# Weights ahead of values, and two hidden-layer steps ahead of the value products, at the start of a fused attention and ELU kernel

## Chip, cores, metric

One core of one Trainium2 chip. The metric is the device time of one execution in microseconds, median of several; all runs quoted here were fast, at a granted TensorE clock of 0.99 to 1.00 over the span.

## The reference

Sliding-window attention (8 batches, 8 heads, 576 positions, head size 64, window 32 to each side), its output laid out as 4608 tokens of 512, then a two-layer network with ELU:

```python
scores = q @ k.T / sqrt(64); keep |i - j| <= 32; attn = softmax(scores)
x = (attn @ v) as [4608, 512]
h = x @ w_in                       # [4608, 2048]
g = where(h > 0, h, exp(min(h, 0)) - 1)
out = g @ w_out                    # [4608, 512]
```

## The kernel before

A hand-scheduled program. Attention works on "pairs" of query blocks (128 tokens each); a tile of the network is 256 tokens, so two pairs. A **step** (kk) is 256 columns of the hidden layer for one tile: eight matmuls into a PSUM tile (h0 or h1 in turn), exponential on ACT, subtraction of 1, and the ELU on DVE, which reads the PSUM tile a last time. The hidden columns of steps 0 and 1 come from the first quarter of w_in, those of steps 2 and 3 from the second. Steps 0 to 3 work on tile 0 (pairs 0 and 1), steps 4 to 7 on tile 1 (pairs 2 and 3). The parts that the change touches:

```python
    # GpSimd's load queue
    load_w_in(0)
    ...                                   # masks
    for m in (3, 4):
        load_v(0, m)
    load_w_in(1)
    load_w_out(0)
    load_w_out(1)
    ...
    # pairs 2 and 3, hung onto the steps ("mid": behind the step's matmuls, "dve": ahead of them)
    at(0, "mid", scores, 2, "s")
    at(0, "mid", scores, 3, "u")
    for i in (2, 3):
        at(0, "mid", exponential, i)                              # ACT
    for i in (2, 3):
        at(0, "mid", rotate_v, 0, 2, VS - 1, (i - 2,))            # DVE copy of values, 64 partitions over
        at(0, "mid", mask, i)                                     # DVE
        at(1, "mid", idle, (4, 2)[i - 2], "y1")                   # dummy matmuls on a tile of zeros
        at(1, "mid", pv, i)                                       # PE: probabilities x values
        at(2, "dve", normalize, i)                                # DVE
        at(3, "mid", x_transpose, i)                              # PE
        at(3, "mid", x_evac, i, nc.scalar)                        # ACT, PSUM -> xT
    at(1, "end", idle, 1, "y1")
    ...
    def mm1(kk):
        ...                                                       # 8 matmuls
            nc.scalar.activation(e_sb, ps, AX.Exp)
            if kk == 1:
                nc.scalar.activation(m_sb, e_sb, AX.Copy, bias=-1.0)
            else:
                nc.vector.tensor_scalar(m_sb, e_sb, -1.0, None, ALU.add)
    ...
    for kk in range(NSTEP + LAG):
        run(kk, "first")
        if 1 <= kk < NSTEP:
            elu(kk - 1)
        run(kk, "dve")
        if kk < NSTEP:
            mm1(kk)
        run(kk, "mid")
        for n in {2: (), 3: (0, 1), 4: (), 5: (2, 3)}.get(
                kk, (kk - LAG,) if kk >= LAG else ()):
            mm2(n)                                                # output products of step n
        run(kk, "end")
```

The softmax here doesn't subtract the row's maximum and nothing guards it: scores larger than these inputs give would overflow.

Of the kernel before, what the change touches and what calls it, by code (L numbers as in the profile page):

```python
# [21 lines left out]
def kernel(  # L22
# [24 lines left out]
    VS = 5  # L47
# [9 lines left out]
    NSTEP = NT * STEPS  # L57
# [36 lines left out]
    def ps_tile(shape, dt, tag, name):  # L94
        return pools[tag].tile(shape, dt, tag=tag, name=name)
# [42 lines left out]
    def load_v(b, m):  # L138
        lo = 128 * m - WIN
        p0 = max(0, -lo)  # L140
        p1 = min(128, S - lo)
        nc.gpsimd.dma_start(  # L142
            out=V_e[b % 3][p0:p1, m, :, 0:D],
            in_=v[b, :, lo + p0:lo + p1, :].rearrange("h p d -> p h d"))
# [28 lines left out]
    def load_w_in(c):  # L173
        w = D_FF // 4
        nc.gpsimd.dma_start(
            out=w_in_sb[:, :, c * w:(c + 1) * w],
            in_=moe_w_in[:, c * w:(c + 1) * w].rearrange(
                "(o p) f -> p o f", p=128))

    def load_w_out(c):  # L180
        n = NFO // 4
        nc.gpsimd.dma_start(
            out=w_out_sb[:, c * n:(c + 1) * n, :],
            in_=moe_w_out[c * n * 128:(c + 1) * n * 128, :].rearrange(
                "(o p) f -> p o f", p=128))
# [46 lines left out]
    def copy_on(eng, d_, s_):  # L232
        if eng is nc.scalar:
            nc.scalar.copy(d_, s_)  # L234
        else:
            eng.tensor_copy(d_, s_)  # L236
# [169 lines left out]
    for mi in (0, 4):  # L406
# [4 lines left out]
        out=masks[:, 3, :], in_=masks[:, 3, :], compare_op=ALU.is_ge,  # L411
        fill=0.0, base=128 - WIN - 1, pattern=[[0, QB]],
        channel_multiplier=-1)
    for m in (3, 4):
        load_v(0, m)
    load_w_in(1)
    load_w_out(0)
    load_w_out(1)

# [49 lines left out]
    def at(kk, slot, fn, *args):  # L469
        tasks.setdefault((kk, slot), []).append((fn, args))  # L470

    def run(kk, slot):
        for fn, args in tasks.get((kk, slot), ()):
            fn(*args)
# [11 lines left out]
    at(0, "mid", scores, 3, "u")  # L486
    for i in (2, 3):
        at(0, "mid", exponential, i)
    for i in (2, 3):
        at(0, "mid", rotate_v, 0, 2, VS - 1, (i - 2,))  # L490
        at(0, "mid", mask, i)

        at(1, "mid", idle, (4, 2)[i - 2], "y1")
        at(1, "mid", pv, i)
        at(2, "dve", normalize, i)
        at(3, "mid", x_transpose, i)
        at(3, "mid", x_evac, i, nc.scalar)
    at(1, "end", idle, 1, "y1")
    at(4, "dve", swap_pools)

    for part, kq in ((HALF_A, 7), (HALF_B, 15)):
# [20 lines left out]
    for i in range(4, NPAIR):  # L522
        two = i >= FIRST_TWO
        kk, z = begin[i], i % 2 if two else 0
# [5 lines left out]
        n = kk + (3 + z if two else 2)  # L530
# [57 lines left out]
    def mm1(kk):  # L588
        t, s = order[kk]
        h = kk % 2  # L590


        tags = (f"h{h}", "s") if kk == NSTEP - 1 else (f"h{h}",)
        w = FG // len(tags)
        psH[kk], m_t[kk] = [], []
        for z, tag in enumerate(tags):
            ps = ps_tile([128, w, TT], FP32, tag, "ps")
            psH[kk].append(ps)
            for j in range(w):
                fo = s * FG + z * w + j  # L600
                for do in range(NDO):
                    nc.tensor.matmul(  # L602
                        ps[:, j, :],
                        lhsT=w_in_sb[:, do, fo * 128:(fo + 1) * 128],
                        rhs=xT[t][:, :, do, :],
                        start=(do == 0), stop=(do == NDO - 1))
        for z, ps in enumerate(psH[kk]):
            e_sb = mpool.tile([128, w, TT], FP32, tag="e_sb", name="e_sb")
            nc.scalar.activation(e_sb, ps, AX.Exp)  # L609
            m_sb = mpool.tile([128, w, TT], BF16, tag="m_sb", name="m_sb")  # L610
            if kk == 1:

                nc.scalar.activation(m_sb, e_sb, AX.Copy, bias=-1.0)
            else:
                nc.vector.tensor_scalar(m_sb, e_sb, -1.0, None, ALU.add)  # L615
            m_t[kk].append(m_sb)
            if kk == NSTEP - 1:
                elu(kk, z)

    def elu(kk, z=0):  # L620
        if z == 0:
            g_t[kk] = mpool.tile([128, FG, TT], BF16, tag="g_sb", name="g_sb",
                                   bufs=5)
        ps = psH[kk][z]
        w = ps.shape[1]
        nc.vector.scalar_tensor_tensor(  # L626
            g_t[kk][:, z * w:(z + 1) * w, :], ps, 0.0, m_t[kk][z],
            ALU.max, ALU.min)
# [3 lines left out]
    def mm2(kk):  # L632
        t, s = order[kk]
        if s == 0:
            psY[t] = [ps_tile([128, D_MODEL], FP32, g, "psY")
                      for g in (("h2", "t0") if t == 1 else ("y0", "y1"))]
        g_sb = g_t.pop(kk)
        last = t == NT - 1 and s == STEPS - 1
        for ts in range(2):
            for j in range(FG):  # L640
                nc.tensor.matmul(  # L641
                    psY[t][ts],
                    lhsT=g_sb[:, j, ts * 128:(ts + 1) * 128],
                    rhs=w_out_sb[:, s * FG + j, :],
                    start=(s == 0 and j == 0),
                    stop=(s == STEPS - 1 and j == FG - 1))
        if s == STEPS - 1:
            for ts in range(2):
                z = 1 - ts if last else ts
                eng = (nc.scalar, nc.vector)[z]  # L650
                y_sb = opool.tile([128, D_MODEL], FP32, tag=f"y_sb{z}",
                                  name="y_sb")
                copy_on(eng, y_sb, psY[t][ts])
                (nc.scalar if last and ts else nc.sync).dma_start(
                    out_t[t, :, ts, :], y_sb)

    LAG = 2
    for kk in range(NSTEP + LAG):
        run(kk, "first")
        if 1 <= kk < NSTEP:  # L660
            elu(kk - 1)
        run(kk, "dve")
        if kk < NSTEP:
            mm1(kk)
        run(kk, "mid")

        for n in {2: (), 3: (0, 1), 4: (), 5: (2, 3)}.get(
                kk, (kk - LAG,) if kk >= LAG else ()):
            mm2(n)
        run(kk, "end")  # L670
# [30 lines left out]
```

## Time and profile before

| | before |
|---|---|
| time, median of the first 3 runs | 305.85 us (305.50 to 306.12) |
| span of the profiled run | 304.2 us |
| step 0 starts on PE | 15.62 us |
| step 4 starts on PE | 25.05 us |
| **front**: step 4's start minus step 0's | **9.43 us** |
| **tail**: from step 4's start to the end of the span | **279.15 us** |

The prediction below shows the lines of the profile that carry these. Two more, from the timeline of PE in the kernel before (start, length, engine, line, operation, output from inputs, shapes, count; in brackets the idle time before and what ended it), give both ends of the front:

```profile
15.62 1.05 PE L602 MATMUL ps<-xT,w_in_sb 128*128 128x256 bf16 x8 [0.80 <-DMA w_in_sb<-in_moe_w_in_dram]
...
25.05 1.91 PE L602 MATMUL ps<-xT,w_in_sb 128*128 128x256 bf16 x16
```

The single instructions that the prediction counts with took, in the kernel before: eight matmuls of 256 columns 0.87 us (L602, 0.109 each), four of 512 columns 0.86 us (L641, 0.215 each; the dummies have this shape and are counted at 0.216), a subtraction on DVE 433 ns (L615, the mean) and on ACT 0.63 us (L613), an ELU on DVE 686 ns (L626, the mean).

### The profile page before, as it was taken

Reading aid. Unit: us, or ns where it says so; the run is one execution under the profiler, and the core shown is the slowest. Engines: PE = TensorE matmul, PEld = TensorE weight load, DVE = VectorE, ACT = ScalarE, POOL = GpSimd, SP = SyncE. Lnnn points to the kernel's source line nnn. Section 1 sums busy time; section 2 is a strip of 40 time slices with the busy share of each in tenths; the row PEclk is TensorE's granted clock in tenths of the full one; section 3 lists DMA queues with packets and bytes.
Section 4 is the critical chain, followed back from the end, with each engine's and each line's share of the span. In section 5 each row is a group of like instructions: output and inputs, shape, how many; then the busy total and the mean of one; then the engine's idle time right before and its main releaser. Section 6 shows DMA issues by size and latency. Waiting matters only on the chain.

```text
span 304.2 us, 7587 instructions
## 1 busy us (share of the span) xinstructions
PE 291.5 (96%) x3038; PEld 197.2 (65%) x3091; DVE 242.1 (80%) x472; ACT 169.0 (56%) x254; POOL 48.7 (16%) x68
## 2 busy tenths in 40 slices
PE   7799999999999999999999999999999999999994
PEld 2466666677666666666666666666666666666662
DVE  6866687978788887988798879887988787877663
ACT  3654656778664566546754675467545454533431
POOL 8836101820004100230023002300000000000000
PEclk9999999999999999999999999999999999999999
DMA  9999999999765987999799969996921111111011
GB/s 191 180 204 205 187 279 401 305 146 213 157 197 145 296 120 217 229 319 147 168 259 316 169 166 260 326 159 125 272 56 71 35 71 35 72 37 69 4 67 70
DMA packets 91973, 52.81 MB, mean 174 GB/s; under 512 B 76578, under 2 KB 81698, under 8 KB 91938
## 3 DMA queue, kind: packets, MB, share of 16 engines
q1 hardware_dynamic: 47186, 35.48, 43.4%
q0 software_dynamic: 42880, 10.10, 42.8%
q10 hardware_dynamic: 1872, 6.75, 6.0%
q8 instruction: 24, 0.39, 0.6%
q14 instruction: 11, 0.09, 0.1%
HBM read 36.70 MB, written 15.34 MB: 171 GB/s over the span
## 4 chain that ended last, share of the span: by engine, by line
PE 89%; DMA 3%; POOL 2%; DVE 2%; issue 2%; ACT 1%; POOLq 0%; DVEq 0%
PE ps L602 41%; PE psY L641 39%; PE psS L336 4%; PE psS L304 3%; DMA w_in_sb<-in_moe_w_in_dram 3%; PE ptx L279 1%; POOL Ve L142 1%; POOL c L136 1%; PE psXT L357 1%; DVE pm L324 0%; DVE g_sb L626 0%; DVE Vo L153 0%; PE ptx L274 0%; ACT e_sb L609 0%; ACT pu L315 0%
## 5 line engine op out<-in xcount | busy, mean ns | idle before, releaser
L609 ACT ACTIVATE e_sb<-ps 128x512 f32<-128x512 f32 (+1 forms) x145 | 86.3, 595 | 120.0 <-PE ps L602 110.4
L602 PE MATMUL ps<-xT,w_in_sb 128*128 128x256 bf16 x1152 | 149.2, 273 | 0.9 <-DMA w_in_sb<-in_moe_w_in_dram 0.8
L641 PE MATMUL psY<-w_out_sb,g_sb 128*128 128x512 bf16 x526 | 139.1, 379 | 3.1 <-issue 0.8
L602 PEld LDWEIGHTS <-w_in_sb 128*128 128x128 bf16 x1152 | 110.8, 98 | 39.0 <-DMA w_in_sb<-in_moe_w_in_dram 1.3
L626 DVE SCALAR_TENSOR_TENSOR g_sb<-ps,m_sb 128x512 bf16<-128x512 f32 (+1 forms) x145 | 99.4, 686 | 12.6
L615 DVE TENSOR_SCALAR m_sb<-e_sb 128x512 bf16<-128x512 f32 x144 | 62.4, 433 | 38.0 <-ACT e_sb L609 36.2
L641 PEld LDWEIGHTS <-g_sb 128*128 128x128 bf16 x576 | 54.6, 98 | 38.6 <-DVE g_sb L626 0.2
L142 POOL DMA_DIRECT2D Ve<-in_v_dram x40 | 35.3, 892 | 139.5 <-PE psS L336 81.4
L315 ACT ACTIVATE pu<-psS 128x1024 bf16<-128x1024 f32 x36 | 36.5, 1020 | 1.5 <-PE psS L304 1.5
L348 DVE TENSOR_TENSOR x_st<-psS,rc 128x512 bf16<-128x512 f32 x36 | 24.9, 692 | 1.2
L324 DVE TENSOR_TENSOR pm<-pu,masks 128x1024 bf16<-128x1024 bf16 x36 | 24.6, 683 | 0.6 <-ACT pu L315 0.5
L234 ACT CAST qkb<-f 128x768 bf16<-128x768 f32 (+1 forms) x29 | 24.9, 860 | 0.0
L336 PEld LDWEIGHTS <-pm 128*64 128x64 bf16 x576 | 11.1, 110 | 9.9 <-DVE pm L324 8.7
L336 PE MATMUL psS<-Ve,pm 128*64 128x65 bf16 x320 | 13.6, 196 | 0.9 <-ACT pu L315 0.8
L236 DVE COPY y_sb<-psY 128x512 f32<-128x512 f32 x18 | 12.3, 685 | 0.9 <-PE psY L641 0.9
L304 PEld LDWEIGHTS <-kT 64*128 64x128 bf16 x576 | 9.6, 95 | 4.9 <-issue 4.0
L336 PE MATMUL psS<-Vo,pm 128*64 128x65 bf16 x256 | 12.0, 196 | 0.2 <-DVE Vo L153 0.2
L304 PE MATMUL psS<-qT,kT 64*128 64x64 bf16 x576 | 11.8, 191 | 0.5 <-DVE kT L236 0.5
L234 ACT COPY y_sb<-psY 128x512 f32<-128x512 f32 x18 | 10.5, 582 | 2.2 <-PE psY L641 2.2
L153 DVE COPY Vo<-Ve 64x1040 bf16<-64x1040 bf16 x24 | 10.7, 447 | 1.1 <-DMA Ve<-in_v_dram 0.4
L395 PE MATMUL ps_idle<-zeros 128*128 128x512 bf16 x24 | 8.3, 455 | 1.4 <-DVE zeros L194 1.3
L234 ACT COPY qT<-ptx 128x1152 bf16<-128x1152 bf16 (+2 forms) x8 | 7.6, 974 | 3.6 <-PE ptx L279 2.8
(36 smaller groups left out, 71.8 us busy)
## 6 DMA issues: line engine op xcount, KB each, us to landing
out_dram<-y_sb SPq DMA_DIRECT2D x35, 256.0 KB, 3.4
f<-in_q_dram SPq DMA_DIRECT2D x12, 576.0 KB, 6.1
f<-in_k_dram SPq DMA_DIRECT2D x12, 576.0 KB, 8.3
in_dram<-qkb ACTq DMA_DIRECT2D x10, 576.0 KB, 4.3
Ve<-in_v_dram POOLq DMA_DIRECT2D x24, 128.0 KB, 11.6
w_in_sb<-in_moe_w_in_dram POOLq DMA_DIRECT2D x4, 512.0 KB, 9.8
w_out_sb<-in_moe_w_out_dram POOLq DMA_DIRECT2D x4, 512.0 KB, 12.7
Ve<-in_v_dram POOLq DMA_DIRECT2D x16, 96.0 KB, 10.1
```

The costliest lines, as they stand in the source:

```text
L142: nc.gpsimd.dma_start(out=V_e[b % 3][p0:p1, m, :, 0:D], in_=v[b, :, lo + p0:lo + p1, :].rearrange("h p d -> p h d"))
L234: nc.scalar.copy(d_, s_)
L304: nc.tensor.matmul(psS[:, h % 2, hp * 128 + z * QB:hp * 128 + (z + 1) * QB], lhsT=kT[b % 2][base:base + 64, KPAD + hp * S + QB * qb - WIN: ...
L315: nc.scalar.activation(pu, _bap(psS, [psS.ap[0], [1, 1024]]), AX.Exp, scale=SCALE)
L324: nc.vector.tensor_mul(pm, pu, _bap(mm, [mm.ap[0], [0, H], [1, 2 * QB]]))
L336: nc.tensor.matmul(psS[QB * z:QB * (z + 1), par, hp * VD:(hp + 1) * VD], lhsT=pm[:, par * HP + hp, z * QB:(z + 1) * QB], rhs=vv[:, qb // 2 ...
L348: nc.vector.tensor_mul(x_st, _bap(psS, [psS.ap[0], [VD, HP], [512, 2], [1, D]]), _bap(rc, [rc.ap[0], [2, HP], [1, 2], [0, D]]))
L602: nc.tensor.matmul(ps[:, j, :], lhsT=w_in_sb[:, do, fo * 128:(fo + 1) * 128], rhs=xT[t][:, :, do, :], start=(do == 0), stop=(do == NDO - 1))
L609: nc.scalar.activation(e_sb, ps, AX.Exp)
L615: nc.vector.tensor_scalar(m_sb, e_sb, -1.0, None, ALU.add)
L626: nc.vector.scalar_tensor_tensor(g_t[kk][:, z * w:(z + 1) * w, :], ps, 0.0, m_t[kk][z], ALU.max, ALU.min)
L641: nc.tensor.matmul(psY[t][ts], lhsT=g_sb[:, j, ts * 128:(ts + 1) * 128], rhs=w_out_sb[:, s * FG + j, :], start=(s == 0 and j == 0), stop=( ...
```

## The change

Its intent: fill PE's wait for values 3 and 4 with steps 2 and 3, which need no values. For that the second quarter of w_in is loaded ahead of these values, the products of pairs 2 and 3 go behind step 3, and the subtractions of steps 2 and 3 join step 1's on ACT, so that DVE has less to do.

```diff
--- before.py
+++ after.py
@@ -411,9 +411,9 @@
         out=masks[:, 3, :], in_=masks[:, 3, :], compare_op=ALU.is_ge,
         fill=0.0, base=128 - WIN - 1, pattern=[[0, QB]],
         channel_multiplier=-1)
+    load_w_in(1)
     for m in (3, 4):
         load_v(0, m)
-    load_w_in(1)
     load_w_out(0)
     load_w_out(1)

@@ -486,16 +486,19 @@
     at(0, "mid", scores, 3, "u")
     for i in (2, 3):
         at(0, "mid", exponential, i)
+        at(1, "dve" if i == 2 else "mid", mask, i)
+        at(3, "dve", rotate_v, 0, 2, VS - 1, (i - 2,))
+        at(3, "mid", pv, i)
+
+    at(1, "mid", idle, 3, "y1")
+    at(3, "dve", idle, 3, "y1")
     for i in (2, 3):
-        at(0, "mid", rotate_v, 0, 2, VS - 1, (i - 2,))
-        at(0, "mid", mask, i)
-
-        at(1, "mid", idle, (4, 2)[i - 2], "y1")
-        at(1, "mid", pv, i)
-        at(2, "dve", normalize, i)
+        at(3, "mid", normalize, i)
+    at(3, "mid", lambda: elu(2))
+    for i in (2, 3):
+        at(3, "mid", lambda n: mm2(n), i - 2)
         at(3, "mid", x_transpose, i)
         at(3, "mid", x_evac, i, nc.scalar)
-    at(1, "end", idle, 1, "y1")
     at(4, "dve", swap_pools)

     for part, kq in ((HALF_A, 7), (HALF_B, 15)):
@@ -608,7 +611,7 @@
             e_sb = mpool.tile([128, w, TT], FP32, tag="e_sb", name="e_sb")
             nc.scalar.activation(e_sb, ps, AX.Exp)
             m_sb = mpool.tile([128, w, TT], BF16, tag="m_sb", name="m_sb")
-            if kk == 1:
+            if 1 <= kk <= 3:

                 nc.scalar.activation(m_sb, e_sb, AX.Copy, bias=-1.0)
             else:
@@ -657,14 +660,14 @@
     LAG = 2
     for kk in range(NSTEP + LAG):
         run(kk, "first")
-        if 1 <= kk < NSTEP:
+        if 1 <= kk < NSTEP and kk != 3:
             elu(kk - 1)
         run(kk, "dve")
         if kk < NSTEP:
             mm1(kk)
         run(kk, "mid")

-        for n in {2: (), 3: (0, 1), 4: (), 5: (2, 3)}.get(
+        for n in {2: (), 3: (), 4: (), 5: (2, 3)}.get(
                 kk, (kk - LAG,) if kk >= LAG else ()):
             mm2(n)
         run(kk, "end")
```

## The prediction

> **What bounds the kernel now.** I read first the page's totals, then the windows view by stages, then the chain of waits and the timeline between 15 and 26 us, where every instruction that the change moves stands.
>
> ```profile
> PE 291.5 (96%) x3038; PEld 197.2 (65%) x3091; DVE 242.1 (80%) x472; ACT 169.0 (56%) x254; POOL 48.7 (16%) x68
> ```
>
> TensorE (PE) is busy for 96% of the span, so only its holes, and work on it that nobody needs, can be won. The windows view says where the holes are:
>
> ```profile
> core 0: us, PE busy (x) PEld busy (x) DVE busy (x) ACT busy (x) POOL busy (x), PEclk, DMA share, GB/s
> 15.62:25.05 9.43, 9.09 (x117) 6.08 (x120) 7.32 (x15) 5.71 (x9) 3.35 (x5) 1.00 1.24 204
> 25.05:45.00 19.95, 19.50 (x204) 13.25 (x206) 14.17 (x28) 10.14 (x15) 5.10 (x6) 1.00 1.46 222
> 45.00:304.20 259.20, 252.12 (x2576) 172.31 (x2620) 209.07 (x405) 145.15 (x220) 26.72 (x30) 1.00 0.86 168
> ```
>
> From 25.05 us on PE is 97 to 98% busy, and the waits view for PE after 25 us names nothing but 0.8 us of "issue" and 0.2 us for one x_st; the other gaps stand where a matmul record is missing. So the instant at which step 4 (the first step of the second token tile) starts on PE, 25.05 us, sets the end: a shift of that start should reach the end one to one. Before it, the chain is this:
>
> ```profile
> 16.70 0.61 ACT e_sb L609
> ...
> 17.33 0.46 DVE m_sb L615
> ...
> 17.83 0.43 DVE Vo L153
> ...
> 18.29 0.69 DVE pm L324
> ...
> 19.01 0.43 DVE Vo L153
> ...
> 19.48 0.42 PE psS L336 x15
> ...
> 21.14 1.75 PE ps L602 x16
> 22.89 0.59 PE psXT L357 x8
> ...
> 25.21 1.75 PE ps L602 x16
> ```
>
> The values' products (L336) wait for VectorE (DVE), which does one rotation (L153) and one mask (L324) at a time; steps 2 and 3 (L602 x16) come after them, at 20.98 in the timeline, 21.14 as the chain counts. Between the last matmul of step 1 (started at 17.17, eight at 0.109 us, so PE is free at 18.05) and step 4 at 25.05 lie 7.00 us. The work in it that is needed: steps 2 and 3, 1.75; 32 value products, about 0.76; 8 x transposes, 0.44; 8 output products, 1.72; sum 4.67. So 2.33 us are dummies (seven at 0.216, 1.51 us) and holes. **2.33 us is all that the change can win, 0.8% of the time.**
>
> The timeline has the three things that decide, and the DMA view the landing of the weights:
>
> ```profile
> 17.20 1.93 ACT L315 ACTIVATE pu<-psS 128x1024 bf16<-128x1024 f32 x2
> 19.00 0.62 ACT L609 ACTIVATE e_sb<-ps 128x512 f32<-128x512 f32 x1
> 19.65 0.63 ACT L613 ACTIVATE m_sb<-e_sb 128x512 bf16<-128x512 f32 x1
> 20.07 1.28 DVE L626 SCALAR_TENSOR_TENSOR g_sb<-ps,m_sb 128x512 bf16<-128x512 f32 x2
> 23.42 1.07 ACT L234 COPY xT<-psXT 128x512 bf16<-128x512 bf16 x2
> ```
>
> ```profile
> w_in_sb<-in_moe_w_in_dram POOLq DMA_DIRECT2D x1, 512.0 KB, 8.9
> Ve<-in_v_dram POOLq DMA_DIRECT2D x1, 96.0 KB, 7.6
> ```
>
> First: step 1's exponential on ScalarE (ACT) stands behind the two score exponentials, its subtraction ends at 20.28, and only then can the ELU of step 1 run. Second: both transposed x tiles are out of PSUM at 24.49, half a microsecond before step 4 asks for them. Third: w_in's second quarter, issued at 10.99, lands at 19.9 us.
>
> [...]eight of L602 take 0.87 us, four of L641 0.86. [...]the first ELU waits behind two masks until 20.07 though its subtraction was done at 17.79. [...]433 ns for L615 against 686 for L626[...] the subtraction is the cheaper half to give away, and ACT pays more for it (0.63). [...]here the first w_in quarter, v3, v4, second w_in quarter landed in the order of issue, at 15.57, 16.7, 17.8 and 19.9.
>
> **The change, part by part.** The instruction order on each engine, which the built kernel shows, is: PE step 1, 3 dummies, step 2, 3 dummies, step 3, 32 value products, output products of step 0, transposes of pair 2, output products of step 1, transposes of pair 3, step 4. DVE: subtraction 0, ELU 0, both masks, ELU 1, both rotations, normalize 2 and 3, ELU 2 and 3. ACT: exponential and subtraction of steps 1, 2, 3 in turn, then both x evictions.
>
> (a) *The load order.* Removed from ahead of the second quarter are v3 and v4, which took 17.8 - 15.57 = 2.2 us of the queue. It then lands near 19.9 - 2.2 = 17.7, v4 near 19.9. Step 2 may start once ELU 0 has freed its PSUM: DVE runs it at 17.85 instead of behind the masks, so by 18.54. Neither holds it: step 2 starts behind the dummies, 18.05 + 3 x 0.216 = 18.70, against 20.98 now, and ends 19.57.
>
> (b) *Step 3* needs the PSUM of step 1, so ELU 1 must be over. Nothing in the change moves ACT's two score exponentials or the exponential and subtraction behind them: 20.28. ELU 1 then runs 20.32 to 21.01 and step 3 starts at 21.05, though the second dummies end at 20.22. A hole of 0.83 us. Step 3 ends 21.05 + 0.87 = 21.92.
>
> (c) *Value products.* The rotations stand behind ELU 1: 20.95 and 21.4, over at 21.85. So the products run 21.93 to 22.7, without a wait. Before, the second set was over at about 20.65.
>
> (d) *Normalizing and transposing.* Now they hide behind steps 2 and 3. After the change only the output products lie beside them: reciprocal and product of pair 2 at 22.6 to 23.6, of pair 3 to 24.4. PE: output products 0 to 23.57, transposes of pair 2 to 23.85, output products 1 to 24.71, transposes of pair 3 start there. In the timeline an eviction starts 0.42 to 0.44 us after the start of such transposes (41.48 and 41.90; 12.82 and 13.26) and takes 0.59, and 0.05 for the hand-over: step 4 starts at 24.72 + 0.43 + 0.59 + 0.05 = **25.79**. A second hole, of about 0.85 us, which the kernel before doesn't have.
>
> (e) *Three subtractions on ACT* (step 1's was there already, so two are new): two times 0.52 us off DVE, two times 0.65 onto ACT, where they lie at about 20.3 and 22.7, ahead of the evictions at 24.2 and 25.15. Off the path on both engines; without them ELU 2 and 3 would end 1 us later, near 26.6, which would touch step 5 only.
>
> Sum: 25.79 - 25.05 = +0.74 us. Crosscheck by contents: 4.67 needed, 6 x 0.216 = 1.30 of dummies, holes of 0.83 and 0.85, together 7.65 from 18.05, which is 25.70. So one dummy (0.22) and a hole of 0.6 are given up for two holes of 1.7. 305.85 + 0.7 is about 306.5.
>
> **The rivals.** *The fill works.* If the x evictions or ELU 1 come sooner than I reckon, the two holes close: 18.05 + 1.30 + 4.67 = 24.02, one microsecond earlier, 304.8. For it speaks that steps 2 and 3 plainly have nothing to do with the values, and that the old chain runs through v3 and v4. Against it speaks that ELU 1 and the third-pair eviction are waits in the built order, each behind a measured serial run on ACT or DVE. Closing just one gives about 305.7.
>
> *The weights stay late.* If the second quarter gains less than the 2.2 us, or the bigger transfer that now follows the first quarter slows its tail, step 2 waits: landing at 19.9 puts step 2 at 19.95, the dummies to 21.47 and step 3 to 21.5, another 0.4 us: 306.9. A first quarter late by 0.2 moves everything by 0.2. Against it: the landings follow the order of issue here, and step 2 has 1.0 us in hand.
>
> *Later loads.* Reused load semaphores make the third w_in quarter wait for v3 instead of v4, and so issue perhaps 1 us later. The queue is then still full with what was issued before it (that quarter took 12.2 us from issue to landing), and it landed at 30.3 against step 8 at 32.73. Hidden: 0.
>
> **Range and chances.** The centre is my sum, 306.5. The low end, 305.7, is one of the two holes closed with the rest as reckoned, or the usual spread of 0.3 on a smaller loss; the high end, 307.1, is a late second quarter or first quarter with 0.2 of spread. A gain of 2% would be 6.1 us, over twice the 2.33 us that are there; a loss of 2% would need a stall that nothing in the order suggests. One in a hundred for each.
>
> **What would show it right or wrong.** Right: step 2 starts on PE near 18.7 and step 3 near 21.05, released by DVE's g_sb; the chain runs through L315 and the exponential and subtraction of step 1 on ACT; step 4 starts near 25.8, released by ACT's eviction of xT, and the last 280 us have the same length. (a) is wrong if step 2 waits for w_in; (b) if step 3 starts within 0.2 of 20.2; (d) if step 4 follows the transposes without a wait. The whole is wrong if step 4 starts before 25.05, or if it starts late and the end doesn't move with it.

## The result, and the profile after

| | before | after |
|---|---|---|
| time, median of 5 | 305.85 us (305.50 to 306.64) | 306.71 us (306.31 to 306.94) |
| ratio of the fast runs | | 1.0022 (95%: 1.0005 to 1.0039) |
| span of the profiled run | 304.2 us | 304.7 us |
| step 0 starts | 15.62 | 15.25 |
| step 4 starts | 25.05 | 25.42 |
| front | 9.43 | **10.17** |
| tail | 279.15 | 279.28 |

A ratio here is the mean time of one kernel's fast runs over the mean of the other's in the same rounds, so it is not quite the ratio of the medians in the table. 0.22% of 305.85 is 0.67 us; the front grew by 0.74. The span grew by only 0.5 because in the profiled run of after the first quarter of w_in happened to land 0.37 us sooner; the tail differs by 0.13.

The totals of the changed kernel, beside those that the prediction shows: PE is "busier" by 3.2 us, but its trace holds 1.7% more matmul records (3090 against 3038) though the program has one matmul fewer, so the row compares nothing.

```profile
PE 294.7 (97%) x3090; PEld 197.0 (65%) x3090; DVE 240.7 (79%) x470; ACT 170.3 (56%) x256; POOL 48.7 (16%) x68
```

The windows view, with the columns of the prediction's fence, for the tail of before and for front and tail of after:

```profile
25.05:304.20 279.15, 271.63 (x2778) 185.56 (x2825) 223.24 (x432) 155.28 (x234) 31.82 (x36) 1.00 0.90 172
```

```profile
15.25:25.42 10.17, 8.95 (x118) 5.97 (x119) 6.90 (x13) 7.06 (x11) 3.80 (x6) 1.00 1.41 197
25.42:304.70 279.28, 274.74 (x2826) 185.35 (x2825) 222.62 (x431) 155.27 (x234) 31.55 (x36) 1.00 0.90 172
```

The tails are alike; all of the difference lies in the front. There PE's timeline of after shows steps 0, 2, 3, the last transposes and step 4:

```profile
15.25 1.05 PE L605 MATMUL ps<-xT,w_in_sb 128*128 128x256 bf16 x8 [0.61 <-DMA w_in_sb<-in_moe_w_in_dram]
...
18.54 1.05 PE L605 MATMUL ps<-xT,w_in_sb 128*128 128x256 bf16 x8
...
20.69 1.03 PE L605 MATMUL ps<-xT,w_in_sb 128*128 128x256 bf16 x8 [0.46 <-DVE g_sb L629]
...
24.36 0.39 PE L357 MATMUL psXT<-ident,x_st 128*128 128x128 bf16 x4
25.42 1.91 PE L605 MATMUL ps<-xT,w_in_sb 128*128 128x256 bf16 x16 [0.67 <-ACT xT L234]
```

Step 2 did move up, from 20.98 to 18.54. Step 3 then waited for DVE's ELU of step 1, and step 4 for ACT's eviction of the last x tile. The idle times in brackets count to the end of a matmul's record, 0.16 us behind the last issue; from issue to issue the holes are 0.62 us (the dummies of 19.42 are through at 20.07) and 0.84 us (the transposes that start at 24.36 are through at 24.58). The waits view of after for PE from 14 to 27 us holds nothing else but step 0's own wait for its weights:

```profile
PE ps L605 <- ACT xT L234: 0.7, 1, 0.7
PE ps L605 <- DMA w_in_sb<-in_moe_w_in_dram: 0.6, 1, 0.6
PE ps L605 <- DVE g_sb L629: 0.5, 1, 0.5
```

What held the two, from the timelines of ACT and DVE of after: the subtraction of step 1, ELU 1 (the ELU of step 1) behind it, and the eviction of the last x tile.

```profile
19.28 0.63 ACT L616 ACTIVATE m_sb<-e_sb 128x512 bf16<-128x512 f32 x1
19.95 0.69 DVE L629 SCALAR_TENSOR_TENSOR g_sb<-ps,m_sb 128x512 bf16<-128x512 f32 x1 [0.46 <-ACT m_sb L616]
24.78 0.59 ACT L234 COPY xT<-psXT 128x512 bf16<-128x512 bf16 x1 [0.50 <-PE psXT L357]
```

ELU 1 ends at 20.64 and step 3 starts at 20.69; the eviction ends at 25.37 and step 4 starts at 25.42. Before, step 1's subtraction ended just as late (20.28, with a step 0 that started 0.37 later), but PE had the value products to do meanwhile.

The loads of after (DMA view of narrow windows; the last number is us from issue to landing): the second quarter of w_in, issued at 9.10, and value 3, issued at 9.86:

```profile
w_in_sb<-in_moe_w_in_dram POOLq DMA_DIRECT2D x1, 512.0 KB, 9.4
Ve<-in_v_dram POOLq DMA_DIRECT2D x1, 128.0 KB, 10.0
```

They landed at 18.5 and 19.9. The page's chain of waits goes another way than ELU 1: through w_out's first quarter, which landed at 22.37, in the same instant as the last value product ended (22.17 + 0.20).

```profile
11.51 10.86 DMA w_out_sb<-in_moe_w_out_dram
...
24.78 0.59 ACT xT L234
```

Two things were due at 22.4 and the chain names one of them. That is a warning for the experiments: taking away what delays the value products will run into this load.

### The profile page after: what moved, and what is told of

It reads as the page before. It is cut to its first block, busy times and chain, and to the rows that moved or that the text cites. A ratio compares the mean times of both kernels' runs of the same rounds, so it can differ in the third digit from the quotient of the medians.

```text
span 304.7 us, 7633 instructions
## 1 busy us (share of the span) xinstructions
PE 294.7 (97%) x3090; PEld 197.0 (65%) x3090; DVE 240.7 (79%) x470; ACT 170.3 (56%) x256; POOL 48.7 (16%) x68
## 4 chain that ended last, share of the span: by engine, by line
PE 89%; DMA 4%; POOL 3%; DVE 1%; ACT 1%; issue 0%; POOLq 0%; DVEq 0%
PE psY L644 41%; PE ps L605 40%; DMA w_out_sb<-in_moe_w_out_dram 4%; PE psS L336 3%; PE psS L304 3%; POOL Ve L142 1%; PE ptx L279 1%; POOL c L136 1%; PE psXT L357 1%; POOL w_in_sb L175 0%; PE ptx L274 0%; ACT pu L315 0%; DVE x_st L348 0%; DVE pm L324 0%; DVE g_sb L629 0%
## 5 line engine op out<-in xcount | busy, mean ns | idle before, releaser
L644 PE MATMUL psY<-w_out_sb,g_sb 128*128 128x512 bf16 x576 | 147.5, 379 | 0.0
L618 DVE TENSOR_SCALAR m_sb<-e_sb 128x512 bf16<-128x512 f32 (+1 forms) x142 | 61.2, 431 | 38.3 <-ACT e_sb L612 36.4
L315 ACT ACTIVATE pu<-psS 128x1024 bf16<-128x1024 f32 x36 | 36.5, 1021 | 1.4 <-PE psS L304 1.4
```

Source lines behind the costliest of these rows:

```text
L315: nc.scalar.activation(pu, _bap(psS, [psS.ap[0], [1, 1024]]), AX.Exp, scale=SCALE)
L644: nc.tensor.matmul(psY[t][ts], lhsT=g_sb[:, j, ts * 128:(ts + 1) * 128], rhs=w_out_sb[:, s * FG + j, :], start=(s == 0 and j == 0), stop=( ...
```

## The experiments

The theory: the loss is the wait for ELU 1 and the wait for the last eviction, less the wait that was removed. The rivals: the load order, the dummies, ACT's added work. In the table all starts are counted from the start of step 0 in the same trace.

| run | step 2 | step 3 | front | tail | ratio to before (95%) |
|---|---|---|---|---|---|
| before | 5.36 | behind it | 9.43 | 279.15 | |
| after | 3.29 | 5.44 | 10.17 | 279.28 | 1.0022 (1.0005 to 1.0039) |
| e9, after again | 3.08 | 5.44 | 10.22 | 279.24 | 1.0022 (1.0000 to 1.0044) |
| e1 values first | 4.16 | 5.69 | 10.32 | 279.24 | 1.0053 (1.0026 to 1.0080) |
| e2 loads only | 9.36 | behind it | 13.51 | 279.18 | 1.0125 (1.0100 to 1.0150) |
| e3 subtractions on DVE | 3.09 | 5.45 | 10.63 | 279.19 | 1.0050 (1.0019 to 1.0080) |
| e4 no dummies | 3.28 | 5.45 | 10.15 | 279.29 | 1.0020 (0.9995 to 1.0044) |
| e5 ELU 1 early | 3.56 | 5.09 | 10.29 | 279.18 | 1.0006 (0.9992 to 1.0021) |
| e6 transposes ahead | 3.35 | 5.44 | 10.07 | 279.23 | 1.0011 (0.9991 to 1.0030) |
| e10, e6 again | 3.07 | 5.43 | 9.83 | 279.23 | 1.0013 (0.9988 to 1.0038) |
| e7 both | 3.09 | 4.67 | 9.28 | 279.15 | 0.9992 (0.9976 to 1.0009) |
| e8 step 2 between | 4.36 | 5.72 | 8.83 | 279.07 | 0.9980 (0.9961 to 0.9998) |
| e11, e8 again | 4.87 | 6.23 | 9.33 | 279.17 | 0.9985 (0.9961 to 1.0009) |

All gave correct results. The tail lies between 279.07 and 279.29 in all thirteen traces, while the front moves by 4.7: **the start of step 4 sets the end**, as predicted.

### e1: values 3 and 4 first again

```diff
 (after)
-    load_w_in(1)
     for m in (3, 4):
         load_v(0, m)
+    load_w_in(1)
```

> The changed kernel with the load order of before: values 3 and 4 ahead of w_in's second quarter, all else kept. I measure the front on PE as the start of step 4 minus the start of step 0: 9.43 us before, 10.17 after. My theory (the loss is the wait for ELU 1 and the wait for the last x eviction): the quarter lands some 4.3 us after step 0 starts instead of 3.3, so step 2 starts 4.35 after step 0, step 3 behind it and the dummies at 5.87 instead of 5.44; front about 10.55, time about 0.4 us above after. Rival (the load order costs the loss, since the values land later): front back to about 9.45 and the time of before.

Front 10.32 and not 9.45, so the new order does not cost the loss; by the time, the change is slower still without it (the 0.15 of front is within what one kernel's traces differ by). Step 2 waits for its weights, as PE's timeline of e1 shows:

```profile
20.00 1.05 PE L605 MATMUL ps<-xT,w_in_sb 128*128 128x256 bf16 x8 [0.91 <-DMA w_in_sb<-in_moe_w_in_dram]
```

That is 4.16 after step 0, not 4.35, and step 3 comes 0.25 later than in after instead of 0.43. The time is 0.9 us above that of after on the same chip (the mean of e1's four runs is 307.50, that of e9's six 306.58), more than the 0.15 of the front. The front doesn't show where the rest lies. In the profiled run step 0 started later (15.84), but the load order does not visibly move that start: w_in's first quarter landed at 14.41 to 15.79 us in the four traces with the values first, at 15.12 to 16.05 in the nine with the weights first.

### e2: the load order alone, on the kernel before

```diff
 (before)
+    load_w_in(1)
     for m in (3, 4):
         load_v(0, m)
-    load_w_in(1)
```

> The kernel before with the load order of after, and nothing else. My theory: values 3 and 4 then land about 4.6 and 5.35 us after step 0 starts, and DVE, which does its work in order, stands at the first rotation: rotation 4.6, mask 5.05, rotation 5.8, mask 6.25, ELU 0 and 1 from 6.9; step 2 starts 7.5 after step 0 instead of 5.36. Front about 11.5, time about 2 us above before. Rival (the values are not what that order waits for): within 0.3 us of before.

Slower by 3.8 us, front 13.51. The direction was right, the size not. DVE stood at the first rotation for 3.08 us until the values were in (first fence, DVE's timeline), and the mask behind it ran only at 20.99, though ACT had finished its input at 18.83; PE was idle from 18.78 to 21.73 meanwhile (second fence, PE's timeline), and then its granted clock was 0.50 (third, windows view of e2, the column behind POOL is the granted clock):

```profile
20.53 0.43 DVE L153 COPY Vo<-Ve 64x1040 bf16<-64x1040 bf16 x1 [3.08 <-DMA Ve<-in_v_dram]
```

```profile
21.73 0.26 PE L336 MATMUL psS<-Ve,pm 128*64 128x65 bf16 x1 [2.96 <-DVE pm L324]
```

```profile
22.00:23.00 1.00, 0.81 (x16) 0.59 (x16) 0.97 (x3) 0.00 (x0) 0.44 (x1) 0.50 1.23 206
23.00:24.00 1.00, 1.00 (x14) 0.32 (x14) 1.00 (x3) 0.00 (x0) 0.62 (x1) 0.50 1.24 206
```

The values came 5.2 us after step 0 instead of 4.6 as I had reckoned, and from 22 to 25 us PE had a granted clock of 0.50 (the same view has 1.00 for 20 to 21 us, 0.85 for 21 to 22, 0.94 for 25 to 26 and 1.00 for 26 to 27). It fell after an idle stretch of 2.96 us. The weights, moved ahead, gained nothing in this trace: they landed 4.28 us after step 0 (4.26 in before).

So the first part of the change makes the second necessary: with the weights ahead, the value products can't stay where they were.

### e3: the subtractions of steps 2 and 3 back on DVE

```diff
 (after)
-            if 1 <= kk <= 3:
+            if kk == 1:
```

> The changed kernel with the subtractions of steps 2 and 3 back on DVE (step 1's stays on ACT, as before). My prediction called these two off the path, touching only step 5: that gives the same front, 10.17. Looking at DVE's order again, the subtraction of step 2 would stand ahead of the rotations and that of step 3 ahead of the normalizing: rotations end 0.5 later, value products start 6.95 after step 0 instead of 6.31, last transposes 9.73; front about 10.8, time 0.6 us above after. The run decides between the two.

Front 10.63, 0.46 above after, so point (e) of the prediction, which had these two off the path, was wrong. DVE's timeline of e3 shows the subtraction of step 2 between ELU 1 and the rotations, and step 3's ahead of the first reciprocal:

```profile
20.99 0.42 DVE L618 TENSOR_SCALAR m_sb<-e_sb 128x512 bf16<-128x512 f32 x1
21.44 1.15 DVE L153 COPY Vo<-Ve 64x1040 bf16<-64x1040 bf16 x2
22.83 0.43 DVE L618 TENSOR_SCALAR m_sb<-e_sb 128x512 bf16<-128x512 f32 x1 [0.24 <-ACT e_sb L612]
```

The last value product starts 7.45 after step 0 against 6.92 in after, 0.53 later, and normalizing and transposes follow it. Not all of that need be the subtractions: the two rotations took 1.15 us here and 0.93 in after, so 0.2 may be the run's (see e6). The times say that the loss is real: the mean of e3's four runs is 307.33, that of e9's six on the same chip 306.58. In this order, moving the two to ACT is worth keeping.

### e4: without the dummies

```diff
 (after)
-    at(1, "mid", idle, 3, "y1")
-    at(3, "dve", idle, 3, "y1")
```

> The changed kernel without the six dummy matmuls around step 2. My theory: step 2 starts when w_in's second quarter lands (3.3 after step 0, as in after), step 3 when ELU 1 is over (5.44), so the dummies stand in the two waits and cost nothing: front 10.17, same time, as long as the clock stays at 1.0. Rival (the dummies delay the steps): front shorter by up to 0.65; rival (without them the clock drops): matmuls of steps 2 and 3 above 0.109 us each, front longer.

Front 10.15: the six dummies stand in waits and cost nothing. The bracket in PE's timeline of e4 shows the wait for ELU 1 grown by them and no earlier start of step 3 (5.45 after step 0):

```profile
21.01 1.03 PE L603 MATMUL ps<-xT,w_in_sb 128*128 128x256 bf16 x8 [1.12 <-DVE g_sb L627]
```

The granted clock stayed at 1.00 through both holes (0.67 us ahead of step 2, 1.12 ahead of step 3): its mean over the span is 1.00, and step 3 took 1.03 us, as in after.

### e5: closing the first hole alone

```diff
 (after)
     for i in (2, 3):
-        at(0, "mid", exponential, i)
-        at(1, "dve" if i == 2 else "mid", mask, i)
+        at(i - 2, "mid", exponential, i)
         at(3, "dve", rotate_v, 0, 2, VS - 1, (i - 2,))
         at(3, "mid", pv, i)
+    at(1, "dve", mask, 2)
+    at(3, "dve", mask, 3)
```

> The changed kernel with the score exponential of pair 3 behind the exponential and subtraction of step 1 on ACT, and its mask behind ELU 1 and the rotations on DVE. This closes the first hole alone: ELU 1 ends about 0.7 us sooner, step 3 starts at about 4.8 after step 0 instead of 5.44. My theory: that alone gives next to nothing, because the rotations still wait for the values (about 4.6 and 5.35), the output products of step 0 still wait for w_out's first quarter (7.1), and the wait for the last x eviction stays: front 10.0 to 10.17. Rival (the wait for ELU 1 is the loss): front about 9.5.

Step 3 came at 5.09 instead of 5.44, without a wait for ELU 1 (step 2's weights, landing at 3.51, kept it from the expected 4.8), and the front was 10.29: nothing won in this trace. What took the hole's place is in PE's timeline of e5:

```profile
22.71 1.02 PE L645 MATMUL psY<-w_out_sb,g_sb 128*128 128x512 bf16 x3 [0.36 <-DMA w_out_sb<-in_moe_w_out_dram]
```

The output products of step 0 waited for w_out's first quarter, 7.28 after step 0. The times disagree: this front would make a ratio of 1.0028, and the timed one is 1.0006 with an interval that ends at 1.0021; the profiled run, 306.59 us, was the slowest of the four. So the trace doesn't show that the first hole is worth nothing, only that this load stands close behind it.

### e6 and e10: closing the second hole alone

```diff
 (after)
-        at(3, "mid", lambda n: mm2(n), i - 2)
+        if i == 2:
+            at(3, "mid", lambda: mm2(0))
         at(3, "mid", x_transpose, i)
         at(3, "mid", x_evac, i, nc.scalar)
+    at(3, "mid", lambda: mm2(1))
```

> The changed kernel with the output products of step 1 behind the transposes of pair 3 instead of ahead of them: they then run while ACT evicts the last x tile. This closes the second hole alone: transposes of pair 3 wait for x_st (8.7 after step 0), output products 8.97 to 9.83, eviction over at 9.8: front about 9.85, time 0.3 us below after. If the eviction is no part of the loss, 10.17 stays.

Front 10.07, a third of the expected 0.32. Its last value product came late (7.14 after step 0, against 6.92 in after), behind two rotations that took 1.19 us together, so I ran it again, beside a second trace of after (e9):

> The same kernel as e6_xtr_ahead, again, because its first profile held two slow rotations on DVE (1.19 us for the two instead of 0.93) that delayed the value products by about 0.2. If that was the run's accident: front about 9.85, time 0.3 below the changed kernel. If 10.05 comes again, the second hole is worth only 0.1.

> The changed kernel itself, unedited, for a second trace and on one chip with the two below. If the front (step 4's start minus step 0's) is a property of the order and not of the run: 10.1 to 10.25 again, and from step 4 to the end 279.1 to 279.3; time 0.6 to 0.9 above before.

e9: front 10.22 and tail 279.24, so after's front repeats within 0.05. e10: front 9.83, 0.34 below the first trace of after and 0.39 below the second; PE went from the output products straight into step 4:

```profile
26.27 1.91 PE L607 MATMUL ps<-xT,w_in_sb 128*128 128x256 bf16 x16
```

In e10 the rotations took 0.88 us, and the last value product started at 6.90. So the second hole is worth 0.3 to 0.4 us when the rotations are quick. Slow ones are no rare accident: they took 1.11 us in e9 and 1.03 in e4 as well, with little harm there, as the output products of step 0 still started at 7.19 and 7.13 (7.16 in after); why one of two equal copies takes up to 0.73 us instead of 0.43 stays open. (In e10 step 0 started at 16.44, after a granted clock of 0.59 from 10 to 12 us and 0.55 from 12 to 14; that is ahead of the front and shows why the front is the better measure.) The times, 1.0011 and 1.0013, agree in direction, and the mean of e10's six runs (306.28) is 0.30 below e9's in the same rounds, as expected; their intervals hold the 1.0022 of after.

### e7: both holes

The edits of e5 and e6 together.

> Both edits together: score exponential of pair 3 behind step 1's ELU input, and transposes of pair 3 ahead of the output products of step 1. My theory: with the value products over sooner, normalizing is over at about 8.35, transposes at 8.6, output products 9.48; front about 9.5, which is the 9.43 of before, time 0.6 to 0.7 us below after. If the two holes are not the loss, the front stays above 9.8.

Front 9.28, a little shorter than before's, and a ratio of 0.9992. Together they give back all of the loss: 0.89 us against after. Some of that is luck. In this trace the output products of step 0 started 6.88 after step 0 without a wait: w_out's first quarter had landed at 6.83, 0.4 sooner than in e5 (7.24). With e5's landing I estimate a front of about 9.7 (7.28, and the 2.40 us that this trace takes from there to step 4), still 0.5 below after. PE's timeline of e7, step 4:

```profile
24.45 1.91 PE L608 MATMUL ps<-xT,w_in_sb 128*128 128x256 bf16 x16
```

**The two holes are the loss**: closing the first alone gave nothing that the front shows, the second 0.1 and 0.3 to 0.4 in two traces, both together most or all of it.

### e8 and e11: what the pieces point to

On the kernel before, with its load order: the useful part of the idea (step 2 needs no values; its subtraction on ACT) without the waits. The first rotation goes ahead of step 0's subtraction, ELU 0 between the masks, step 2 between the two sets of value products (its weights land at about that time), and step 3 behind them, where it covers the normalizing.

```diff
 (before)
     for i in (2, 3):
         at(0, "mid", exponential, i)
+    at(0, "dve", rotate_v, 0, 2, VS - 1, (0,))
+    at(0, "mid", rotate_v, 0, 2, VS - 1, (1,))
+    at(0, "mid", mask, 2)
+    at(1, "dve", mask, 3)
+    at(1, "mid", idle, 4, "y1")
+    at(1, "mid", pv, 2)
+    at(1, "mid", idle, 2, "y1")
+    at(2, "mid", pv, 3)
+    for i in (2, 3):
+        at(2, "mid", normalize, i)
     for i in (2, 3):
-        at(0, "mid", rotate_v, 0, 2, VS - 1, (i - 2,))
-        at(0, "mid", mask, i)
-        at(1, "mid", idle, (4, 2)[i - 2], "y1")
-        at(1, "mid", pv, i)
-        at(2, "dve", normalize, i)
         at(3, "mid", x_transpose, i)
         at(3, "mid", x_evac, i, nc.scalar)
-    at(1, "end", idle, 1, "y1")
+        at(3, "mid", lambda n: mm2(n), i - 2)
 ...
-            if kk == 1:
+            if 1 <= kk <= 2:
 ...
-        for n in {2: (), 3: (0, 1), 4: (), 5: (2, 3)}.get(
+        for n in {2: (), 3: (), 4: (), 5: (2, 3)}.get(
```

> A version of my own on the kernel before, with its load order (values first): the first rotation ahead of step 0's subtraction on DVE, ELU 0 between the two masks, step 2 between the value products of pair 2 and pair 3, step 3 behind them (it covers the normalizing), step 2's subtraction on ACT, and each of the output products 0 and 1 behind a pair's transposes. Worked out from the trace of before: value products of pair 2 at 3.4 after step 0 instead of 3.41 to 3.86, step 2 at 4.35 when its weights land, pair 3 at 5.2, step 3 at 5.6, last transposes near 7.8, step 4 at about 8.8 to 8.9: front 0.55 to 0.65 shorter than the 9.43 of before, time about 305.2. If the values or DVE hold it instead, 9.4 or more.

> The same kernel as e8_step2_between, again, with five rounds and beside the changed kernel on one chip: front 8.8 to 8.9, time 0.5 to 0.7 below before and 1.2 to 1.4 below the changed kernel. If the first result was luck of the rounds, its interval will hold 1.0 here.

Front 8.83 in e8, as worked out, and no wait of PE in the front at all (PE's timeline of e8, steps 2 and 4):

```profile
19.56 1.05 PE L606 MATMUL ps<-xT,w_in_sb 128*128 128x256 bf16 x8
...
24.03 1.91 PE L606 MATMUL ps<-xT,w_in_sb 128*128 128x256 bf16 x16
```

In e11 it was 9.33: value 3 was in only 1.85 after step 0 (DVE's first rotation at 17.05), against 0.69 in e8 (15.89), and everything behind it slid. So this order is open to the landing of the values, which the run decides; with e11's landing its front is only 0.10 below that of before. The times: 305.44 us median against 306.08 of before (ratio 0.9980, 0.9961 to 0.9998), then 305.47 against 305.61 (0.9985, 0.9961 to 1.0009). Both point the same way and one interval holds 1.0, so a gain of 0.5 us over before is likely and not proven. Against the changed kernel on the same chip, in the same rounds, the mean of e11's runs (305.42) is 1.15 us below that of e9's (306.58). Its medians are the lowest of the versions tried.

## Why the prediction was right

Every start below is counted from the start of step 0 (15.62 in before, on which the prediction is built; 15.25 in after).

| step of the prediction | predicted | measured |
|---|---|---|
| (a) second quarter of w_in lands | 2.1 | 3.3 |
| (a) step 2 starts | 3.08 | 3.29 |
| (b) step 3 starts, behind ELU 1 | 5.43 | 5.44 |
| (c) value products start | 6.31 | 6.41 |
| (d) output products of step 0 | 7.1 | 7.16 |
| (d) last transposes | 9.10 | 9.11 |
| (d) step 4 starts, behind the eviction | 10.17 | 10.17 |
| sum: change of the front | +0.74 | +0.74 |
| time | 306.5 | 306.71 |

- **The sum** came out to 0.01 us, which is luck: the second trace of the changed kernel (e9) gives +0.79, the front of before comes from one trace, and two things that the prediction didn't have (a late step 2, and a load due when the value products ended) happened to cost nothing.
- **The bound** (step 4's start sets the end one to one): right; the tail is the same within 0.22 us in thirteen traces.
- **(a) the load order**: right in direction, mis-sized. The term "v3 and v4, which took 2.2 us of the queue" gave the weights 1.0 us (4.3 after step 0 in before, 3.3 in after). It read the differences between landings as the share of each transfer, and they are not that when the order changes. Other traces with the weights first show 2.9 to 3.5 (2.3 in e10, where step 0 itself was late), and e2 4.3, no gain at all. Step 2 waited about 0.2 us for it (not at all in e9, where it started at 3.08). That did no harm because step 3 was held by ELU 1; it is what the rival "the weights stay late" said, at half its size.
- **(b) ELU 1**: right. e4 (dummies taken away, step 3 unmoved) and e5 (exponential moved, step 3 earlier) confirm what holds it.
- **(c), (d)**: right, to 0.1 us; e10 confirms the second hole's cause and size. The 0.1 in (c) is a slip: it starts the rotations at 20.95 though it has ELU 1 end at 21.01. The crosscheck has one too: the holes of before are 2.33 - 1.51 = 0.82 us, not 0.6, so that 1.7 of holes for 0.82 and a dummy makes about +0.65, as 25.70 says.
- **(e) the subtractions**: wrong. The step that failed is "Off the path on both engines; without them ELU 2 and 3 would end 1 us later, near 26.6, which would touch step 5 only". On DVE they would stand ahead of the rotations and of the normalizing, on the path; e3 measured 0.46 us, of which 0.2 may be its slow rotations. It didn't touch the sum, as the change has them on ACT.
- **Later loads**: the third quarter of w_in was issued 2.0 us later (20.17, behind v3's landing at 19.9, against 18.13, behind v4's at 17.8), not 1; hidden, as said: the waits view of after for PE from 26 us on names no load, only 0.2 us for one x_st.
- **What would show it**: step 2 near 18.7, step 3 near 21.05, step 4 near 25.8 held (with this run's 0.37 taken into account). "The chain runs through L315 and the exponential and subtraction of step 1" didn't in the first trace: the chain names w_out's first quarter, which landed together with the last value product, and which I had not among the waits. In the second trace (e9), where that load landed at 6.99, the chain does run through L315 and step 1's exponential and subtraction.
- **A comparison that shows only so much**: L626, set against L615, reads two tensors, one of them in PSUM. Its 686 ns against 433 tell which instruction is the longer one, not which of these two differences costs the time.
- **The rival "the fill works"**: fell. e5 and e7 show what it would have needed: both waits closed.

What stays open: the 0.7 us by which e1's time exceeds what its front shows, why rotations are slow in some runs, and what sets the landing of step 0's weights, which differed by up to 1.6 us between profiled runs (14.41 to 16.05). That it makes up most of the spread of the times is likely and not shown, as only one run of each label was profiled.

## What to carry to other kernels

Work that "needs nothing" can still need a free accumulator (here step 3 waited 0.46 us for ELU 1 to free its PSUM tile): before you pull a step forward, write down who frees its buffer, and when, and whether the work it replaces was itself the cover for something later. Here PE's idle time before the values was filled, and the normalizing and the evictions that had been hidden behind the moved steps came to light (0.67 us of waiting for the last one). And give a change of a few tenths of a microsecond a measure of its own inside the trace, from one event to another, instead of the time of the whole.

## What else the traces show

- The clock: in e2 the granted clock was 0.50 from 22 to 25 us, after an idle stretch of PE of 2.96 us; in e4 it stayed at 1.00 through holes of 0.67 and 1.12 us. In e10 it was 0.59 on average from 10 to 12 us and 0.55 from 12 to 14, with PE busy for 1.94 and 2.00 us of these; what brought it down there is not shown.
- The spacing of matmuls: four of 512 columns took 0.86 us, 215 ns each, and eight of 256 columns 0.87 us, 109 ns each.
- The loads: these four, issued by GpSimd, landed in the order of issue, in before (w_in's first quarter 15.57, v3 16.7, v4 17.8, second quarter 19.9) and in after (first quarter 15.2, second 18.5, v3 19.9, v4 20.7). What one of them gains by being issued earlier is another matter: moved ahead of two loads, the later of which had landed 2.2 us behind the first quarter, the second quarter of w_in gained 1.0 us in after and nothing in e2, and in after these two lost 3.5 and 3.2 (v3 from 1.1 to 4.6, v4 from 2.2 to 5.4 after step 0's start).
- The spread of the landings from run to run: the first quarter of w_in landed between 14.41 and 16.05 us in thirteen traces.
